# Routing products on whole 128x128 stationary tiles in a fused attention and two-stage expert kernel

## The chip, the cores and the metric

One core of one Trainium2 chip runs the whole kernel in one launch. The metric is device time in microseconds; the kernel before took 1211.03 us, the median of three runs.

## What is computed

The reference is an attention with two kinds of masks, then a layer of eight experts that each take exactly their share of tokens, then a layer of four experts that every token passes, mixed by given weights. The change touches the routing of the first expert layer alone:

```python
    logits = x @ w_gate                      # 2304 tokens, 8 experts
    order = np.argsort(-flat)
    ...
        if assigned[tok] >= 0 or counts[e] >= cap:      # cap = 2304 // 8 = 288
            continue
        assigned[tok] = e
    ...
    for e in range(E):
        mask = assigned == e
        h = np.maximum(x[mask] @ w1[e], 0.0)
        out[mask] = h @ w2[e]
```

## The kernel before, in words

Tokens lie as 128 partitions times 18 columns (NC). Routing goes in eight turns, g = 0 to 7. In each, `search` (line 552) finds the logit threshold at which the next expert fills up: every token's best remaining logit m and its one-hot expert oh (`best`, line 516), then rounds of a search over the bits of the threshold. A round compares m with up to 128 candidate thresholds (G, `reach`, line 529), counts per expert on TensorE how many tokens reach each candidate (line 595 in turn 0, 18 products; line 601 in turns 1 to 6, 9 products of two token columns each), lets VectorE count the candidates at which an expert is full (sat), spreads that to all partitions by a product with sat as stationary operand (line 608, in the last round followed by line 610), and sets the next bits. Turn 0 takes its first counts in the front already (`first_count`, line 543, product in line 545). Turns 0 to 6 have six rounds each; in turns 1 to 6 rounds one and two have 64 candidates of which 63 are counted (126 columns for two token columns), three more 31 (62 columns), the last 32 (64 columns). Turn 7 takes what is left without a search. Each turn ends with a prefix count (lines 655 and 656, both with a full 128x128 stationary tile), which gives each token its place.

`place` (line 677) turns places into a list of token indices: a one-hot W of 18 columns per token column, multiplied on TensorE with the one-hot O (line 696, 18 products), a copy to tk, and three fp32 products with K["rad"] (line 703, each issued as two), cast to idx. Then GpSimd gathers the tokens' rows (line 891), TensorE transposes them (line 908; line 915 in turn 0), and ScalarE and VectorE split them in a high and a low part (xh, xl) for the expert's products.

Stationary operands of the routing are narrow: 8 columns in line 545 and 595, 40 in line 601, 18 in line 696; in line 608 they stand on 8 partitions, in line 610 on 1, in line 703 on 18 partitions with 32 columns.

`experts` (line 750) issues the products of both expert layers (lines 971 and, later, 1201; all 128x128 stationary, moving 256, 288 or 512 columns in fp32r). The order on every engine is written out when the program is built. After each expert product `tick` (line 955) advances a planned TensorE time and lets the two chains, `chain_a` (searches) and `chain_b` (placements and gathers), emit their next piece when it is due. Routing products don't count in that planned time; VectorE operations count by their shapes. So the pieces of turns 1 to 7 stand between the expert products in one queue of TensorE, from about 160 to 610 us. Turn 0 runs before the first expert's products, between transposes of attention rows (lines 276 and 287) that are stored for the gather.

Of the kernel before, what the change touches and what calls it, by code (L numbers as in the profile page):

```python
# [18 lines left out]
FT = mybir.dt.float32  # L19
# [436 lines left out]
def route_consts(nc, cst):  # L456
    K = {}
    tok = cst.tile([128, NC], I32, name="tok")
    nc.gpsimd.iota(tok[:, :16], pattern=[[576, 4], [256, 2], [1, 2]], base=0, channel_multiplier=2)
    for b in range(4):  # L460
        nc.gpsimd.iota(tok[32 * b:32 * b + 32, 16:], pattern=[[1, 2]], base=576 * b + 512, channel_multiplier=2)
    vi = cst.tile([128, NC, 2], I32, name="vi")
    nc.vector.tensor_scalar(vi[:, :, 0], tok, 8, None, op0=OP.arith_shift_right)
    nc.vector.tensor_scalar(vi[:, :, 1], tok, 255, None, op0=OP.bitwise_and)
    K["vals"] = cst.tile([128, NC, 2], BF, name="vals")
    nc.vector.tensor_copy(K["vals"], vi)
    K["w8"] = cst.tile([128, 8], FT, name="w8")
    nc.gpsimd.iota(K["w8"], pattern=[[-1, 8]], base=8, channel_multiplier=0, allow_small_or_imprecise_dtypes=True)
    K["w8b"] = cst.tile([1, 8], BF, name="w8b")
    nc.gpsimd.iota(K["w8b"], pattern=[[-1, 8]], base=-8, channel_multiplier=0, allow_small_or_imprecise_dtypes=True)  # L470
    jj = cst.tile([128, 128], I32, name="jj")
    nc.gpsimd.iota(jj, pattern=[[1, 128]], base=0, channel_multiplier=0)
    K["jsh"], K["id8"] = {}, {}
    one_f = cst.tile([8, 8], FT, name="one_f")
    nc.gpsimd.memset(one_f, 1.0)
    i8 = cst.tile([8, 8], FT, name="i8")
    nc.gpsimd.affine_select(i8, one_f, pattern=[[-1, 8]], base=0, channel_multiplier=1, compare_op=OP.is_equal, fill=0.0)
    for nb, sh, first in ((7, 25, True), (6, 26, True), (6, 20, False), (5, 15, False), (5, 10, False), (5, 5, False), (5, 0, False)):
        n = 1 << nb
        t = cst.tile([128, n], I32, name=f"jsh{sh}")  # L480
        nc.vector.tensor_scalar(t, jj[:, :n], sh, None, op0=OP.logical_shift_left)
        if first:
            a = cst.tile([128, n], I32, name=f"ja{sh}")
            nc.vector.tensor_scalar(t, t, INT_MIN, None, op0=OP.bitwise_xor)
            nc.vector.tensor_scalar(a, t, 31, 0x7FFFFFFF, op0=OP.arith_shift_right, op1=OP.bitwise_and)
            nc.vector.tensor_tensor(t, t, a, OP.bitwise_xor)
            nc.vector.memset(t.bitcast(FT)[:, 0:1], -3.0e38)
        K["jsh"][sh] = t
        s = cst.tile([8, 8], BF, name=f"id8_{sh}")
        nc.vector.tensor_scalar(s, i8, 1.0 if first else float(1 << sh) if sh else 16.0, None, op0=OP.mult)  # L490
        K["id8"][sh] = s
    K["ones"] = cst.tile([128, 128], BF, name="ones")
    nc.gpsimd.memset(K["ones"], 1.0)
    K["ntri"] = cst.tile([128, 128], BF, name="ntri")
    nc.gpsimd.memset(K["ntri"], -1.0)
    nc.gpsimd.affine_select(K["ntri"], K["ntri"], pattern=[[-1, 128]], base=0, channel_multiplier=1, compare_op=OP.is_ge, fill=0.0)
    K["j32"] = cst.tile([128, 32], I32, name="j32")
    nc.gpsimd.iota(K["j32"], pattern=[[1, 32]], base=0, channel_multiplier=0)
    K["k9"] = cst.tile([128, 9], I32, name="k9")
    nc.gpsimd.iota(K["k9"], pattern=[[1, 9]], base=-32, channel_multiplier=0)  # L500
    K["zeros"] = cst.tile([128, 2 * NC], FT, name="zeros")
    nc.gpsimd.memset(K["zeros"], 0.0)
    radix = cst.tile([18, 3, 3, 2], FT, name="radix")
    nc.gpsimd.iota(radix, pattern=[[0, 9], [-255, 2]], base=256, channel_multiplier=0, allow_small_or_imprecise_dtypes=True)
    rsel = cst.tile([18, 3, 3, 2], FT, name="rsel")
    nc.gpsimd.affine_select(rsel, radix, pattern=[[-2, 3], [-6, 3], [-1, 2]], base=0, channel_multiplier=1, compare_op=OP.is_equal, fill=0.0)
    K["rad"] = cst.tile([18, 3, 3], FT, name="rad")
    nc.vector.tensor_reduce(K["rad"], rsel, AX.X, OP.add)
    K["first"] = [cst.tile([128, NC], FT, name="m0"), cst.tile([128, NC], FT, name="mw0"), cst.tile([128, NC, 32], BF, name="oh0"),
                  cst.tile([128, NC, 8], FT, name="eq0")]  # L510
    nc.vector.memset(K["first"][2], 0.0)
    K["cnt"] = cst.tile([8, 128], FT, name="cnt0")
    return K


# [24 lines left out]
    reach(nc, K["first"][0], K["jsh"][25].bitcast(FT), G, c0, c1, 128)  # L540


def first_count(nc, K, G, p, c0, c1):
    for c in range(c0, c1):
        nc.tensor.matmul(p[:8, :127], K["first"][2][:, c, :8], G[:, c - c0, 1:128], start=c == c0, stop=c == c1 - 1)
    if c0 == 0:
        nc.vector.tensor_copy(K["cnt"][:, :127], p[:8, :127])
    elif c0 < 14:
        nc.vector.tensor_tensor(K["cnt"][:, :127], p[:8, :127], K["cnt"][:, :127], OP.add)


def search(nc, K, wk, ps, L, g, S, out):
# [5 lines left out]
    if g < 7:  # L558
# [5 lines left out]
        for r, (nb, sh) in enumerate(rounds):  # L564
# [1 line left out]
            lo = 0 if sh == 0 else 1  # L566
            nxt = rounds[r + 1] if sh else None
            p = ps.tile([128, 128], FT, name="pa")
            sat = wk.tile([8, 1], BF, name="sat")
            junk = wk.tile([8, 128], FT, name="junk")  # L570
            if g == 0 and r == 0:
                G = wk.tile([128, 4, 128], BF, name="G")
# [7 lines left out]
            else:  # L580
# [11 lines left out]
                yield "d"  # L592
                if g == 0:
                    for c in range(NC):
                        nc.tensor.matmul(p[:8, lo:n], oh[:, c, :8], G[:, c, lo:n], start=c == 0, stop=c == NC - 1)
                    yield "p"
                    nc.vector.tensor_scalar(junk[:, lo:n], p[:8, lo:n], float(CAP), 0.0, op0=OP.is_ge, op1=OP.add, accum_out=sat)
                else:
                    pp = p[:, :2 * n].rearrange("p (a n) -> p a n", a=2)[:, :, lo:]
                    for c in range(0, NC, 2):  # L600
                        nc.tensor.matmul(pp[:40], oh[:, c:c + 2, :].rearrange("p a e -> p (a e)")[:, :40], G[:, c:c + 2, lo:n], start=c == 0, stop=c == NC - 2)  # L601
                    yield "p"
                    need = wk.tile([8, 64], FT, name="need")
                    nc.vector.tensor_scalar(need[:, lo:n], pp[32:40, 1], -1.0, float(CAP), op0=OP.mult, op1=OP.add)
                    nc.vector.scalar_tensor_tensor(junk[:, lo:n], pp[:8, 0], 0.0, need[:, lo:n], op0=OP.add, op1=OP.is_ge, accum_out=sat)
            yield "d"
            p = ps.tile([128, 8], FT, name="pa")
            nc.tensor.matmul(p, sat.to_broadcast([8, 128]), K["id8"][sh], start=True, stop=sh > 0)
            if sh == 0:
                nc.tensor.matmul(p, K["ones"][:1], K["w8b"], start=False, stop=True)  # L610
            yield "P"
            d = wk.tile([128, 1], I32, name="d", bufs=2)
            nc.vector.tensor_reduce(d, p, AX.X, OP.max)
# [63 lines left out]
def place(nc, K, wk, ps, out):  # L677

    pm = out["pm"]
    kj = wk.tile([128, 2, NC], I32, name="kj")  # L680
    nc.vector.tensor_scalar(kj[:, 0], pm, 5, None, op0=OP.arith_shift_right)
    nc.vector.tensor_scalar(kj[:, 1], pm, 31, None, op0=OP.bitwise_and)
    yield "q"
    O = wk.tile([128, NC, 32], BF, name="O")
    W9 = wk.tile([128, NC, 9], BF, name="W9")
    W = wk.tile([128, NC, 9, 2], BF, name="W")
    nc.vector.tensor_tensor(W9, K["k9"][:, None, :].to_broadcast([128, NC, 9]), kj[:, 0, :, None].to_broadcast([128, NC, 9]), OP.is_equal)
    pi = ps.tile([128, 32], FT, name="pb")
    for c0 in (0, 9):
        s = slice(c0, c0 + 9)  # L690
        yield "q"
        nc.vector.tensor_tensor(O[:, s], K["j32"][:, None, :].to_broadcast([128, 9, 32]), kj[:, 1, s, None].to_broadcast([128, 9, 32]), OP.is_equal)
        nc.vector.tensor_tensor(W[:, s], W9[:, s, :, None].to_broadcast([128, 9, 9, 2]), K["vals"][:, s, None, :].to_broadcast([128, 9, 9, 2]), OP.mult)
    yield "d"
    for c in range(NC):
        nc.tensor.matmul(pi[:18], W[:, c].rearrange("p k v -> p (k v)"), O[:, c], start=c == 0, stop=c == NC - 1)
    yield "p"
    tk = wk.tile([18, 32], FT, name="tk")
    nc.vector.tensor_copy(tk, pi[:18])
    yield "d"  # L700
    pi = ps.tile([128, 3], FT, name="pb")
    for b in range(3):
        nc.tensor.matmul(pi[32 * b:32 * b + 32], tk, K["rad"][:, b], start=True, stop=True)
    yield "p"
    idx = wk.tile([96, 3], I32, name="idx", bufs=2)
    nc.vector.tensor_copy(idx, pi[:96])
    out["idx"] = idx
# [673 lines left out]
```

## Time and profile before

| | us |
|---|---|
| median of 3 runs | 1211.03 |
| lowest and highest | 1208.41, 1212.58 |
| profiled execution, its time | 1208.96 |
| its span, first to last instruction | 1207.2 |
| TensorE busy in it (share of the span) | 1177.4 (98%) |
| VectorE | 853.9 (71%) |
| ScalarE | 621.8 (52%) |
| GpSimd | 422.9 (35%) |

PE is TensorE's products, PEld its weight loads, DVE VectorE, ACT ScalarE, POOL GpSimd, SP the engine that issues most DMAs. Records of products overlap and their ends are modelled, so the distance between starts tells more than their lengths. The span is what the trace shows; the median is over other executions of the same program.

### The profile page before, as it was taken

The page shows a single profiled execution, that of the slowest core. Times are in us where ns is not written, and L with a number is a line of the kernel's source. Part 1 is how long each engine was busy: PE and PEld are TensorE (multiplying, and loading weights), DVE is VectorE, ACT ScalarE, POOL GpSimd, SP SyncE. Part 2 cuts the span into 40 slices and gives each one's busy share as a digit, 9 for nine tenths or more (in the row PEclk, how much of TensorE's full clock was granted, in tenths as well). Part 3 has the DMA queues.
Part 4 walks back from the last instruction along what each step waited for, and adds up shares of the span by engine and source line. Part 5 has one row for each costly group of instructions (what it writes and reads, how often), then busy time and mean ns, then how long its engine had stood idle before and what let it go on. Part 6 is the DMA issues. An engine that isn't in the chain of part 4 may idle for free.

```text
span 1207.2 us, 24909 instructions
## 1 busy us (share of the span) xinstructions
PE 1177.4 (98%) x9088; PEld 1038.6 (86%) x9095; DVE 853.9 (71%) x2248; ACT 621.8 (52%) x1602; POOL 422.9 (35%) x453
## 2 busy tenths in 40 slices
PE   9999799999999999999999999999999999999997
PEld 6777588898888888899999988999888999899996
DVE  5777677777785877778765588767877766766673
ACT  5898455542441442455545455555555555555552
POOL 4343030100000101001012565565755556756553
PEclk9999899999999999999999999999999999999999
DMA  8761564553252452475665433333433333333320
GB/s 187 181 151 39 172 203 147 163 166 99 88 160 81 136 156 56 141 226 170 191 204 156 127 90 102 98 100 102 125 103 89 105 105 105 123 106 102 98 81 36
DMA packets 191955, 152.98 MB, mean 127 GB/s; under 512 B 27640, under 2 KB 158776, under 8 KB 191400
## 3 DMA queue, kind: packets, MB, share of 16 engines
q1 hardware_dynamic: 188664, 141.74, 40.2%
q0 software_dynamic: 3168, 9.65, 2.5%
q8 instruction: 71, 1.16, 0.4%
q14 instruction: 52, 0.43, 0.1%
HBM read 141.77 MB, written 9.58 MB: 125 GB/s over the span
## 4 chain that ended last, share of the span: by engine, by line
PE 82%; DVE 7%; issue 3%; ACT 3%; DMA 2%; POOL 2%; SPq 0%; POOLq 0%; DVEq 0%; ACTq 0%
PE o L971 35%; PE h L971 18%; PE h L1201 16%; DVE wl L746 3%; DMA raw<-in_moe_w_dram 2%; PE tr L164 2%; PE pt L222 1%; PE pa L601 1%; PE tr L153 1%; PE av L242 1%; PE s L186 1%; PE av L235 1%; ACT hh L864 1%; POOL wl L1190 1%; DVE u L746 1%
## 5 line engine op out<-in xcount | busy, mean ns | idle before, releaser
L746 DVE TENSOR_TENSOR wl<-raw,wh 128x512 fp32r<-128x512 f32 x352 | 272.0, 804 | 4.6 <-ACT wh L844 3.8
L971 PE MATMUL o<-wl,hh 128*128 128x512 f32 x576 | 227.8, 395 | 0.0
L971 PE MATMUL o<-wh,hh 128*128 128x512 f32 x576 | 227.7, 395 | 0.0
L971 PE MATMUL o<-wh,hl 128*128 128x512 f32 x576 | 226.5, 393 | 0.0
L864 ACT ACTIVATE hh<-h 128x256 fp32r<-128x256 f32 (+1 forms) x208 | 81.7, 393 | 241.2 <-PE h L971 221.4
L844 ACT CAST wh<-raw 128x512 fp32r<-128x512 f32 x272 | 160.0, 619 | 59.8 <-DMA raw<-in_moe_w_dram 57.7
L1190 POOL TENSOR_TENSOR wl<-raw,wh 128x512 fp32r<-128x512 f32 x96 | 122.5, 1298 | 194.8 <-ACT wh L1189 194.7
L746 DVE SCALAR_TENSOR_TENSOR hl<-h,hh 128x256 fp32r<-128x256 f32 (+1 forms) x208 | 89.8, 432 | 103.6 <-ACT hh L864 102.4
L891 POOL DMA_INDIRECT xg<-xd,idx x24 | 26.3, 1095 | 367.0 <-DVE idx L746 285.0
L971 PEld LDWEIGHTS o<-wh,hl 128*128 128x128 f32 x576 | 108.6, 188 | 23.3
L1201 PE MATMUL h<-hold,wh 128*128 128x256 f32 x640 | 120.9, 282 | 1.4 <-DVE u L746 1.1
L1201 PEld LDWEIGHTS h<-hold,wh 128*128 128x128 f32 x640 | 107.9, 188 | 15.8 <-DVE u L746 2.8
L746 DVE SCALAR_TENSOR_TENSOR hl<-u,hh 128x256 fp32r<-128x256 f32 x144 | 83.0, 576 | 46.5 <-ACT hh L864 46.5
L1176 ACT CAST wh<-sums 128x512 fp32r<-128x512 f32 x96 | 59.8, 622 | 106.9 <-POOL sums L1164 70.6
L971 PEld LDWEIGHTS o<-wl,hh 128*128 128x128 f32 x576 | 108.6, 189 | 6.0
L971 PEld LDWEIGHTS o<-wh,hh 128*128 128x128 f32 x576 | 108.5, 188 | 6.1
L864 ACT ACTIVATE hh<-u 128x256 fp32r<-128x256 f32 x144 | 59.9, 416 | 103.3 <-DVE u L746 103.2
L746 DVE TENSOR_TENSOR u<-h,u 128x256 f32<-128x256 f32 x144 | 60.2, 418 | 62.9 <-PE h L1201 55.5
L746 DVE TENSOR_TENSOR wl<-sums,wh 128x512 fp32r<-128x512 f32 x96 | 74.7, 779 | 36.7 <-ACT wh L1176 36.7
L1201 PE MATMUL h<-hold,wl 128*128 128x256 f32 x320 | 89.8, 281 | 0.0
L971 PE MATMUL h<-xh,wh 128*128 128x288 f32 x256 | 76.1, 297 | 0.0
L971 PE MATMUL o<-hh,wl 128*128 128x288 f32 x256 | 76.0, 297 | 0.0
(271 smaller groups left out, 2927.2 us busy)
## 6 DMA issues: line engine op xcount, KB each, us to landing
raw<-in_moe_w_dram SPq DMA_DIRECT2D x464, 256.0 KB
vl<-in_v_dram SPq DMA_DIRECT2D x16, 192.0 KB
ql<-in_q_dram SPq DMA_DIRECT2D x4, 576.0 KB
kl<-in_k_dram SPq DMA_DIRECT2D x4, 576.0 KB
qs<-in_q_dram SPq DMA_DIRECT2D x3, 576.0 KB
ks<-in_k_dram SPq DMA_DIRECT2D x3, 576.0 KB
xd<-y SPq DMA_DIRECT2D x2, 576.0 KB
xd<-hl SPq DMA_DIRECT2D x5, 192.0 KB
```

Source lines behind the costliest of these rows:

```text
L153: nc.tensor.transpose(p[:, 72 * a:72 * a + 72], src[:, r:r + 2, :].rearrange("p r d -> p (r d)"), ident[:72, :72])
L164: nc.tensor.matmul(p[64 * x:64 * x + 64, 96 * t:96 * t + 96], src[:, 2 * hp + x, 3 * a + t, :], ident[:96, :96], start=True, stop=True)
L186: nc.tensor.matmul(out[:rows], lt, rt, start=True, stop=True)
L222: nc.tensor.transpose(p[:keys, rows * j:rows * j + rows], T["p"][:rows, j, :keys], ident[:rows, :rows])
L746: return f(*args, **kw)
L844: nc.scalar.copy(c["h"][:, sl], c["raw"][a])
L864: nc.scalar.activation(hi, src, AF.Relu)
L891: nc.gpsimd.indirect_dma_start(out=xg[:, k, :], out_offset=None, in_=xd, in_offset=bass.IndirectOffsetOnAxis(ap=idx[:, k:k + 1], axis=0))
L971: nc.tensor.matmul(out, a, b, start=start, stop=stop)
L1176: nc.scalar.copy(S["W"][nm][0], src[nm]())
L1190: nc.gpsimd.tensor_tensor(l, r, h.bitcast(FT), OP.subtract)
L1201: mmx = lambda o, a, b, first, lastm, n: (nc.tensor.matmul(o, a, b, start=first, stop=lastm, skip_group_check=True), tick(n / 2315 + 0.009))
```

## The change

Every narrow stationary operand becomes 128 partitions by 128 columns. In `search` the columns of oh are taken four token columns at a time (32 each), of which the results read only the first; oh gets three more token columns. sat becomes a constant tile of 128 partitions that is zero but for the first 8; the small constants are made on 128 partitions (zero outside their old part; a fill is added for w8b). In `place` W and tk become constant tiles with zeros behind (and before) their old part, filled once by GpSimd in the first placement; line 703's three products become three accumulating ones over a shifting window of tk. Moving columns, VectorE's operations and the order of the pieces stay.

```diff
-    K["w8b"] = cst.tile([1, 8], BF, name="w8b")
-    nc.gpsimd.iota(K["w8b"], pattern=[[-1, 8]], base=-8, channel_multiplier=0, allow_small_or_imprecise_dtypes=True)
+    K["w8b"] = cst.tile([128, 8], BF, name="w8b")
+    nc.gpsimd.memset(K["w8b"], 0.0)
+    nc.gpsimd.iota(K["w8b"][:1], pattern=[[-1, 8]], base=-8, channel_multiplier=0, allow_small_or_imprecise_dtypes=True)
...
-    K["first"] = [cst.tile([128, NC], FT, name="m0"), cst.tile([128, NC], FT, name="mw0"), cst.tile([128, NC, 32], BF, name="oh0"),
+    K["first"] = [cst.tile([128, NC], FT, name="m0"), cst.tile([128, NC], FT, name="mw0"), cst.tile([128, NC + 3, 32], BF, name="oh0"),
...
+    K["sat"] = cst.tile([128, 1], BF, name="sat")
+    nc.vector.memset(K["sat"], 0.0)
...
+def whole(oh, c):
+    return oh[:, c:c + 4, :].rearrange("p a e -> p (a e)")
...
-        nc.tensor.matmul(p[:8, :127], K["first"][2][:, c, :8], G[:, c - c0, 1:128], start=c == c0, stop=c == c1 - 1)
+        nc.tensor.matmul(p[:, :127], whole(K["first"][2], c), G[:, c - c0, 1:128], start=c == c0, stop=c == c1 - 1)
...
-            sat = wk.tile([8, 1], BF, name="sat")
+            sat = K["sat"][:8]
...
-                        nc.tensor.matmul(p[:8, lo:n], oh[:, c, :8], G[:, c, lo:n], start=c == 0, stop=c == NC - 1)
+                        nc.tensor.matmul(p[:, lo:n], whole(oh, c), G[:, c, lo:n], start=c == 0, stop=c == NC - 1)
...
-                        nc.tensor.matmul(pp[:40], oh[:, c:c + 2, :].rearrange("p a e -> p (a e)")[:, :40], G[:, c:c + 2, lo:n], start=c == 0, stop=c == NC - 2)
+                        nc.tensor.matmul(pp, whole(oh, c), G[:, c:c + 2, lo:n], start=c == 0, stop=c == NC - 2)
...
-            nc.tensor.matmul(p, sat.to_broadcast([8, 128]), K["id8"][sh], start=True, stop=sh > 0)
+            nc.tensor.matmul(p, K["sat"].to_broadcast([128, 128]), K["id8"][sh], start=True, stop=sh > 0)
             if sh == 0:
-                nc.tensor.matmul(p, K["ones"][:1], K["w8b"], start=False, stop=True)
+                nc.tensor.matmul(p, K["ones"], K["w8b"], start=False, stop=True)
...
-    W = wk.tile([128, NC, 9, 2], BF, name="W")
+    if "W" not in K:
+        K["W"] = wk.tile([128, NC * 18 + 110], BF, name="W")
+        nc.gpsimd.memset(K["W"][:, NC * 18:], 0.0)
+        K["tk"] = wk.tile([128, 224], FT, name="tk")
+        nc.gpsimd.memset(K["tk"], 0.0)
+    W = K["W"][:, :NC * 18].rearrange("p (c k v) -> p c k v", c=NC, v=2)
...
-        nc.tensor.matmul(pi[:18], W[:, c].rearrange("p k v -> p (k v)"), O[:, c], start=c == 0, stop=c == NC - 1)
+        nc.tensor.matmul(pi, K["W"][:, 18 * c:18 * c + 128], O[:, c], start=c == 0, stop=c == NC - 1)
     yield "p"
-    tk = wk.tile([18, 32], FT, name="tk")
-    nc.vector.tensor_copy(tk, pi[:18])
+    nc.vector.tensor_copy(K["tk"][:18, 96:128], pi[:18])
...
-        nc.tensor.matmul(pi[32 * b:32 * b + 32], tk, K["rad"][:, b], start=True, stop=True)
+        nc.tensor.matmul(pi, K["tk"][:, 96 - 32 * b:224 - 32 * b], K["rad"][:, b], start=b == 0, stop=b == 2)
```

## Rows read from the trace of the kernel before

**Rows 1.** Stage table: length, then busy PE, PEld, DVE, ACT, POOL; clock; DMA

```profile
160.00:610.00 450.00, 444.74 (x3321) 400.14 (x3321) 336.07 (x944) 197.69 (x425) 31.80 (x32) 1.00 0.48 145
```

**Rows 2.** Chain of waits in 160 to 610 us, shares of the stage by line

```profile
by line: PE h L971 41.5%; PE o L971 40.7%; PE pa L601 3.3%; DMA raw<-in_moe_w_dram 3.2%; DVE wl L746 1.9%; ACT wh L844 1.6%; PE pb L908 1.1%; DVE G L746 0.9%; PE pb L696 0.8%; PE pa L608 0.8%; issue 0.8%; DVE xl L746 0.6%; DVE hl L746 0.6%; 
```

**Rows 3.** Timeline of PE, one line 608 product: start, length, instruction (us)

```profile
167.44 0.29 PE L971 MATMUL h<-xl,wh 128*128 128x288 f32 x1
167.67 0.17 PE L608 MATMUL pa<-id,sat 8*128 8x8 bf16 x1
167.78 0.40 PE L971 MATMUL h<-xh,wl 128*128 128x288 f32 x1
168.01 0.29 PE L971 MATMUL h<-xh,wh 128*128 128x288 f32 x1
168.14 0.29 PE L971 MATMUL h<-xl,wh 128*128 128x288 f32 x1
```

**Rows 4.** Timeline of PE, the full-tile pair of lines 655 and 656

```profile
515.01 0.29 PE L971 MATMUL h<-xh,wh 128*128 128x288 f32 x1
515.14 0.19 PE L655 MATMUL pa<-st,ntri 128*128 128x36 bf16 x1
515.18 0.18 PE L656 MATMUL pa<-cum,ones 128*128 128x36 bf16 x1
515.21 0.38 PE L971 MATMUL h<-xl,wh 128*128 128x288 f32 x1
515.43 0.29 PE L971 MATMUL h<-xh,wl 128*128 128x288 f32 x1
```

**Rows 5.** Timeline of PE, a group of line 601 with 126 columns

```profile
171.58 0.29 PE L971 MATMUL h<-xh,wh 128*128 128x288 f32 x1
171.81 0.68 PE L601 MATMUL pa<-G,oh 128*40 128x126 bf16 x9
...
172.65 0.29 PE L971 MATMUL h<-xh,wl 128*128 128x288 f32 x1
```

**Rows 6.** Timeline of PE, a group of line 601 with 62 columns

```profile
176.51 0.30 PE L971 MATMUL o<-hh,wl 128*128 128x288 f32 x1
176.74 0.44 PE L601 MATMUL pa<-G,oh 128*40 128x62 bf16 x9
...
177.34 0.29 PE L971 MATMUL o<-hl,wh 128*128 128x288 f32 x1
```

**Rows 7.** Timeline of PE, a group of line 696

```profile
338.31 0.29 PE L971 MATMUL o<-hh,wl 128*128 128x288 f32 x1
338.52 0.61 PE L696 MATMUL pb<-O,W 128*18 128x32 bf16 x18
...
339.30 0.29 PE L971 MATMUL h<-xl,wh 128*128 128x288 f32 x1
```

**Rows 8.** Timeline of PE, a group of line 703

```profile
341.02 0.30 PE L971 MATMUL o<-hh,wl 128*128 128x288 f32 x1
341.24 0.23 PE L703 MATMUL pb<-rad,tk 18*32 18x3 f32 x6
...
341.64 0.29 PE L971 MATMUL o<-hl,wh 128*128 128x288 f32 x1
```

**Rows 9.** Timeline of PE in the front, line 340

```profile
59.07 0.31 PE L340 MATMUL xr<-four,lg 128*128 128x16 f32 x2
```

**Rows 10.** Groups of instructions, 160 to 610 us, line 908: busy us, mean ns | idle before it, releaser

```profile
L908 PE MATMUL pb<-ident,xg 96*128 96x96 f32 x72 | 10.2, 250 | 4.3 <-DVE xl L746 4.3
```

**Rows 11.** Timeline of all engines, end of the first placement; brackets: idle before, releaser

```profile
145.02 0.41 PE L696 MATMUL pb<-O,W 128*18 128x32 bf16 x9 [0.20 <-DVE W L746]
...
146.04 0.16 DVE L746 CAST idx<-pb 96x3 int32<-96x3 f32 x1 [0.39 <-PE pb L703]
...
147.16 1.03 POOL L891 DMA_INDIRECT xg<-xd,idx  x1 [30.17 <-DMA raw<-in_moe_w_dram]
```

**Rows 12.** Timeline of POOL at the start, a small fill

```profile
3.81 0.13 POOL L502 MEMSET zeros<- 128x36 f32 x1
```

More of the change, by code (lines that the diff above doesn't have):

```diff
@@ L473, in route_consts @@
     K["jsh"], K["id8"] = {}, {}
-    one_f = cst.tile([8, 8], FT, name="one_f")
+    one_f = cst.tile([128, 8], FT, name="one_f")
     nc.gpsimd.memset(one_f, 1.0)
-    i8 = cst.tile([8, 8], FT, name="i8")
+    i8 = cst.tile([128, 8], FT, name="i8")
     nc.gpsimd.affine_select(i8, one_f, pattern=[[-1, 8]], base=0, channel_multiplier=1, compare_op=OP.is_equal, fill=0.0)
@@ L488, in route_consts @@
         K["jsh"][sh] = t
-        s = cst.tile([8, 8], BF, name=f"id8_{sh}")
+        s = cst.tile([128, 8], BF, name=f"id8_{sh}")
         nc.vector.tensor_scalar(s, i8, 1.0 if first else float(1 << sh) if sh else 16.0, None, op0=OP.mult)
@@ L502, in route_consts @@
     nc.gpsimd.memset(K["zeros"], 0.0)
-    radix = cst.tile([18, 3, 3, 2], FT, name="radix")
+    radix = cst.tile([128, 3, 3, 2], FT, name="radix")
     nc.gpsimd.iota(radix, pattern=[[0, 9], [-255, 2]], base=256, channel_multiplier=0, allow_small_or_imprecise_dtypes=True)
-    rsel = cst.tile([18, 3, 3, 2], FT, name="rsel")
+    rsel = cst.tile([128, 3, 3, 2], FT, name="rsel")
     nc.gpsimd.affine_select(rsel, radix, pattern=[[-2, 3], [-6, 3], [-1, 2]], base=0, channel_multiplier=1, compare_op=OP.is_equal, fill=0.0)
-    K["rad"] = cst.tile([18, 3, 3], FT, name="rad")
+    K["rad"] = cst.tile([128, 3, 3], FT, name="rad")
     nc.vector.tensor_reduce(K["rad"], rsel, AX.X, OP.add)
-    K["first"] = [cst.tile([128, NC], FT, name="m0"), cst.tile([128, NC], FT, name="mw0"), cst.tile([128, NC, 32], BF, name="oh0"),
+    K["first"] = [cst.tile([128, NC], FT, name="m0"), cst.tile([128, NC], FT, name="mw0"), cst.tile([128, NC + 3, 32], BF, name="oh0"),
                   cst.tile([128, NC, 8], FT, name="eq0")]
```

## The prediction, made before the changed kernel was run

> **What bounds the kernel now.** I read the stage table first. Between 160 and 610 us, where seven of the eight searches and placements run among the products of the experts, TensorE is busy 444.74 of 450 us at full granted clock, VectorE 336.07 [rows 1]. Then the chain of waits of that stage: 41.5% and 40.7% of it are the experts' products, and the routing's own products stand in it too, line 601 with 3.3% (14.9 us), lines 696 and 608 with 0.8% each [rows 2]. Line 608's 0.8% is 3.6 us, 36 rounds at 0.10 us, which is the 0.11 us from its start to the next product's [rows 3]: nearly all of its rounds lie on the chain. So TensorE's time in the routing counts here. The rest of the chain is mostly weight loads from memory (3.2%), VectorE and ScalarE.
>
> What a routing product costs is read from starts in the timeline, since records overlap. Products of 288 columns start 0.13 us apart. With one line 608 product among them (8 rows x 128 columns stationary) the last product before starts at 167.44 and the second after at 168.01: 0.57 us where two steps are 0.26, so it adds 0.31 us [rows 3]. It starts 0.10 us later than its turn, and the second product after is late by another 0.10. Now the kernel's own full-tile pair, lines 655 and 656, same types, 128x128 stationary, 36 columns: from 515.01 to 515.43 is 0.42 us, so **two** of them add 0.16 us. The first comes on its turn (0.13), the second 0.04 later, the next product 0.03 after that [rows 4]. The partial tile costs a wait on both sides that the full one doesn't.
>
> **The change part by part.** A full-tile product alone is taken at 0.16 - 0.04 = 0.12 us, each further one in a group at the larger of 0.04 us (the pair's step) and its own streaming. Line 601's groups of nine last 0.68 us with 126 columns [rows 5] and 0.44 with 62 [rows 6]; with the last record near 0.19, as 36 columns have [rows 4], the short ones step by (0.44 - 0.19) / 8 = 0.03 us, the long ones by 0.03 more, 0.06. Counts are from the loops: six searches of six rounds after 160 us, two rounds of 126 columns and four of 62 or 64 in each; seven placements.
>
> Saturation product (608), 36 rounds: 0.31 becomes 0.12, saves 0.19 each, 6.8 us. Line 610, in one round of six, keeps its step and is counted at nothing: it stands behind 608 in the same group.
>
> Line 601, 126 columns, 12 groups: 171.58 to 172.65 is 1.07, less 0.26, adds 0.81 [rows 5]. After: 0.12 + 8 x 0.06 + 0.03 for the longer last one = 0.63. Saves 0.18 each, 2.2 us.
>
> Line 601, 62 or 64 columns, 24 groups: 176.51 to 177.34 is 0.83, adds 0.57 [rows 6]. After: 0.12 + 8 x 0.04 = 0.44. Saves 0.13 each, 3.1 us. Here the wider load takes part back (0.04 for 0.03).
>
> Line 696, 18 products, 7 placements: 338.31 to 339.30 is 0.99, adds 0.73 [rows 7]. After: 0.12 + 17 x 0.04 = 0.80. **Costs** 0.07 each, 0.5 us.
>
> Line 703, six issues of three fp32 products: 341.02 to 341.64 is 0.62, adds 0.36 [rows 8]. No row shows a stream of full fp32 tiles with 3 columns. Two of line 340 (full fp32, 16 columns) take 0.31 us together [rows 9], one full fp32 product lasts 0.25 [rows 10], so their step is 0.06. After: 0.12 + 5 x 0.06 = 0.42, costs 0.06 each, 0.4 us. Bounds are 0.04 (the bf16 pair, rows 4) and 0.11 (a load after a drain, rows 3): from a gain of 0.3 to a loss of 2.2 us. I take the value next to line 340, which has the same type and tile.
>
> Sum: 6.8 + 2.2 + 3.1 - 0.5 - 0.4 = **11.2 us** of TensorE's time after 160 us. Not all of it reaches the end: where the chain runs through loads, ScalarE and VectorE, TensorE waits anyway, as at the transposes of gathered tokens (4.3 us idle behind VectorE's xl [rows 10]). TensorE's lines make 41.5 + 40.7 + 3.3 + 1.1 + 0.8 + 0.8 = 88% of that chain [rows 2], so I take 0.88 x 11.2 = 9.9 us. Bounds are 11.2 (all of it) and some 3.5 (rival two).
>
> The first search and placement, before 155 us, I cost at nothing, between a loss and a gain of 0.8 us. Five saturation products save up to 5 x 0.19 and the groups of line 595 give some back by their loads, as line 696 does. In the placement a stationary tile now reaches into later columns of W, so 16 products instead of 9 wait for the second half of W (the record of those nine is 0.41 us [rows 11]): 7 more at 0.04 to 0.11 us and wider ones, and the three fp32 products, make the indices 0.5 to 1.6 us later. Hidden behind: the index cast ends at 146.20 and the first gather starts at 147.16, released by a DMA that landed [rows 11], so 0.96 us of delay costs nothing; without that cover it goes straight into the gather, on which the first expert waits. The line 545 counts save at most a wait or two in the front. The two fills of the placement's pads come on GpSimd, which is idle for 30.17 us before that gather [rows 11]; the added fill at the start is one like line 502's, 0.13 us [rows 12], ahead of masks that nobody needs in the first microseconds. Were these covers gone, each costs its 0.13. No wait on VectorE's queue is added: it reads the same corners of the results, and the order written by the pacing doesn't count routing products.
>
> The profiled execution took 1208.96 us, span 1207.2; the median is 1211.03, 2.1 above it. 1208.96 - 9.9 = 1199.1, on the median **1201.1 us**.
>
> **The rivals.** One: the load of 128 columns isn't wholly covered. The pair's 0.04 is one step, not a stream of nine. With a load covered only in part, a step of 126 columns lies between 0.06 (covered) and 0.10 (0.06 + 0.04). The page TensorE: Matmul & The Clock Gate of the Trainium skill, section Back-to-back issue gap, gives some 81 ns for a sustained load and product of 128 columns; no row here shows such a stream. At 0.08, and 0.055 and 0.05 for the shorter ones, line 601 saves 12 x 0.02 + 24 x 0.01 = 0.5, line 696 loses 7 x 0.24 = 1.7, line 703 0.4, 608 keeps its 6.8: 5.2 x 0.88 = 4.6 us, 1206.5. For it: nine different loads in a row. Against: the expert products load 128 fp32 columns for each 0.13 us step without a trace of it [rows 3].
>
> Two: VectorE and the weight loads take over. They have 0.75 of the stage busy and own stretches of the chain. If two thirds of the gain is waited away again at xl and at the loads, 3.7 us is left, 1207.3. Against: those stretches begin with a product that itself comes earlier.
>
> Three, the other side: a wide load costs what it costs after a drain, 0.11 us each [rows 3], in every group of the search and the placement. Then a long group is 0.12 + 8 x 0.11 + 0.03 = 1.03, loses 0.22 x 12 = 2.6; a short one 1.00, loses 0.43 x 24 = 10.3; line 696 1.99, loses 1.26 x 7 = 8.8; line 703 0.31 x 7 = 2.2; with 6.8 gained that is 17.1 lost, 15 on the chain, 1226. It decides from a step of 0.071 us, where the sum is zero. The rule that speaks for it is in the Trainium skill, TensorE: Matmul & The Clock Gate, section LDWEIGHTS (loading the stationary operand): a load's time goes by its columns, 1.2 in a nanosecond, by which 128 would take an estimated 107 ns and 40 take 33. The pair's step of 0.04 [rows 4] speaks against it, so I hold to the sum of 11.2.
>
> Four: the change doesn't do what it says, because the wait belongs to the change of type (bf16 among fp32) and not to the tile. Then wider loads cost 2 to 3 us and nothing is saved, 1213.5. Rows 4 have the same change of type and no wait on entry.
>
> **How the numbers follow.** Forecast 0.73, rival one 0.10, two 0.08, three 0.05, four 0.04. About 0.3%, 3.6 us, is what a measurement can tell from no change. Faster: 0.73 + 0.10 + half of two = 0.87; same: the other half and rival four, 0.08; slower: rival three, 0.05. Range: low 1196.5, with the whole 11.2 us, the upper bounds of line 703 and of the first placement and an execution as far under the median as the profiled one; high 1207.5, which takes in rivals one and two.
>
> **What would show it.** Right: line 608 starting 0.12 to 0.13 us after the product before it, the next product 0.03 behind; groups of line 601 near 0.51 us with 62 columns; line 696's group longer than 0.61 us; TensorE's idle time at xl a little larger than 4.3. Wrong: line 601's steps over 0.07 us, a start still 0.10 late, or the same stage length with longer waits for raw and xl.

## The result and the profile after

The changed kernel takes 1197.42 us (median of 4 runs, 1195.12 to 1198.43), the kernel before, run beside it, 1211.2. The ratio is 0.9894, 95% interval 0.9877 to 0.991: faster by 1.1%, where 0.8% was forecast. The profiled execution took 1198.43 us, the longest of the four.

The page of the changed kernel, span and busy time:

```profile
span 1196.7 us, 24923 instructions
...
PE 1167.4 (98%) x9095; PEld 1040.1 (87%) x9095; DVE 852.7 (71%) x2249; ACT 622.0 (52%) x1602; POOL 424.1 (35%) x456
```

The stage table of 160 to 610 us, columns as in [rows 1]:

```profile
160.00:610.00 450.00, 444.07 (x3402) 410.94 (x3402) 343.57 (x959) 203.57 (x438) 35.07 (x34) 1.00 0.50 152
```

TensorE is as full as before and still at full granted clock, but 3402 of its products now lie in the same 450 us, against 3321 [rows 1]. It does the same work with less waiting between its products.

The timeline of PE in the changed kernel (start, length, instruction, us): a saturation product (now line 615), a count of 126 columns and one of 62 (line 608), a placement (708) and its index products (714), each with its neighbours among the experts' products:

```profile
168.56 0.29 PE L982 MATMUL h<-xl,wh 128*128 128x288 f32 x1
168.69 0.18 PE L615 MATMUL pa<-id,sat 128*128 128x8 bf16 x1
168.73 0.38 PE L982 MATMUL h<-xh,wl 128*128 128x288 f32 x1
168.95 0.29 PE L982 MATMUL h<-xh,wh 128*128 128x288 f32 x1
...
177.27 0.29 PE L982 MATMUL o<-hh,wl 128*128 128x288 f32 x1
177.41 0.44 PE L608 MATMUL pa<-G,oh 128*128 128x62 bf16 x9
177.68 0.38 PE L982 MATMUL o<-hh,wh 128*128 128x288 f32 x1
177.90 0.29 PE L982 MATMUL o<-hl,wh 128*128 128x288 f32 x1
...
247.23 0.29 PE L982 MATMUL o<-hh,wh 128*128 128x288 f32 x1
247.37 0.68 PE L608 MATMUL pa<-G,oh 128*128 128x126 bf16 x9
247.85 0.38 PE L982 MATMUL o<-hl,wh 128*128 128x288 f32 x1
248.07 0.29 PE L982 MATMUL o<-hh,wl 128*128 128x288 f32 x1
...
334.18 0.29 PE L982 MATMUL o<-hh,wl 128*128 128x288 f32 x1
334.32 0.61 PE L708 MATMUL pb<-O,W 128*128 128x32 bf16 x18
334.78 0.38 PE L982 MATMUL h<-xh,wh 128*128 128x288 f32 x1
335.00 0.29 PE L982 MATMUL h<-xl,wh 128*128 128x288 f32 x1
...
336.71 0.30 PE L982 MATMUL o<-hh,wl 128*128 128x288 f32 x1
336.85 0.73 PE L714 MATMUL pb<-rad,tk 128*128 128x3 f32 x6
337.43 0.38 PE L982 MATMUL o<-hh,wh 128*128 128x288 f32 x1
337.65 0.30 PE L982 MATMUL o<-hl,wh 128*128 128x288 f32 x1
```

Read by starts, as before. The saturation product starts on its turn, 0.13 us behind 168.56, and the next product 0.04 later; from 168.56 to 168.95 is 0.39, so it adds 0.13 where it added 0.31 [rows 3]. The two counts, read the same way, add 0.63 less 0.26, 0.37, where it was 0.57, and 0.84 less 0.26, 0.58, where it was 0.81 [rows 5, 6]. The records' lengths tell nothing of this: the 62-column group lasts 0.44 in both kernels, and so does the 126-column one with 0.68 [rows 5, 6]. What went are the waits before and behind them. The placement, which I thought would grow, adds 334.18 to 335.00 less 0.26, 0.56, against 0.73 [rows 7]. The index products alone grew: 336.71 to 337.65 is 0.94, adds 0.68, against 0.36 [rows 8].

Done for all groups between 160 us and the last placement, medians of the added time in us (for the last column, times the count). A group's added time runs from the start of the product before it to the start of the second product behind it, less the steps that these two neighbours have without it (0.13 us with 288 columns, 0.12 with 256, 0.23 with 512):

| group | count | before | predicted | changed | saved, us |
|---|---|---|---|---|---|
| saturation | 36 | 0.305 | 0.12 | 0.126 | 6.4 |
| counts, 126 columns | 12 | 0.81 | 0.63 | 0.57 | 2.9 |
| counts, 62 or 64 | 24 | 0.57 | 0.44 | 0.367 | 4.9 |
| placement | 7 | 0.74 | 0.80 | 0.555 | 1.3 |
| index products | 7 | 0.38 | 0.42 | 0.687 | -2.1 |

Together 13.4 us of TensorE's time, for the 11.2 of the prediction. To see what of it reaches the end I take the stretch from the first count after the front to the last index product, by the first and last starts of their lines. Those of the kernel before, then of the changed one:

```profile
L601 PE MATMUL pa<-G,oh x324: 193/193/233, 164.3 to 504.4; 128*40 128x62 bf16 x84, 128*40 128x126 bf16 x54, 128*40 128x64 bf16 x24
...
L703 PE MATMUL pb<-rad,tk x48: 167/187/209, 145.7 to 607.7; 18*32 18x3 f32 x48
```

```profile
L608 PE MATMUL pa<-G,oh x324: 189/193/230, 165.5 to 494.0; 128*128 128x62 bf16 x84, 128*128 128x126 bf16 x54, 128*128 128x64 bf16 x24
...
L714 PE MATMUL pb<-rad,tk x48: 166/252/373, 147.2 to 597.1; 128*128 128x3 f32 x48
```

443.4 us (164.3 to 607.7) became 431.6 (165.5 to 597.1): 11.8 of the 13.4 us arrive. Behind the stage the two traces stay a constant distance apart: 10.6 us at the last index product, 10.5 at the end of the span. What the stage's chain of waits and TensorE's waits show of the rest, first the chain's shares by line, then who TensorE waited for (us in total, times, longest):

```profile
by line: PE h L982 39.3%; PE o L982 38.4%; DMA raw<-in_moe_w_dram 6.9%; PE pa L608 2.4%; DVE wl L757 1.8%; ACT wh L855 1.6%; PE pb L919 1.1%; issue 0.9%; DVE G L757 0.9%; PE pb L714 0.8%; PE pb L708 0.7%; DVE xl L757 0.7%; DVE hl L757 0.6%; 
```

```profile
PE pb L919 <- DVE xl L757: 3.7, 6, 1.2
PE pa L615 <- DVE junk L757: 0.8, 1, 0.8
...
PE o L982 <- DVE hold L757: 0.5, 1, 0.5
```

Saturation no longer stands in the chain's list and the counts fell from 3.3% to 2.4% [rows 2]; weight loads rose from 3.2% to 6.9%, so the chain now passes through them more often, yet TensorE hardly idles more: its waits over 50 ns in the stretch sum to 5.9 us against 5.3. The wait at xl was 4.3 [rows 10] and is 3.7 here; new are one for the search's own VectorE result ahead of a saturation product (0.8) and one at the combination of the experts' outputs (hold, 0.5).

### The profile page after: what moved, and what is told of

Its sections match the earlier page's. It is cut to its first block, busy times and chain, and to the rows that moved or that the text cites. A ratio compares the mean times of both kernels' runs of the same rounds, so it can differ in the third digit from the quotient of the medians.

```text
span 1196.7 us, 24923 instructions
## 1 busy us (share of the span) xinstructions
PE 1167.4 (98%) x9095; PEld 1040.1 (87%) x9095; DVE 852.7 (71%) x2249; ACT 622.0 (52%) x1602; POOL 424.1 (35%) x456
## 4 chain that ended last, share of the span: by engine, by line
PE 79%; DVE 6%; DMA 6%; issue 3%; ACT 3%; POOL 2%; SPq 1%; POOLq 0%; DVEq 0%; ACTq 0%
PE o L982 34%; PE h L982 17%; PE h L1212 17%; DMA raw<-in_moe_w_dram 3%; DVE wl L757 2%; PE tr L164 1%; PE pt L222 1%; PE av L242 1%; PE pa L608 1%; DMA kl<-in_k_dram 1%; DMA ks<-in_k_dram 1%; DMA vl<-in_v_dram 1%; POOL wl L1201 1%; PE s L186 1%; ACT hh L875 1%
## 5 line engine op out<-in xcount | busy, mean ns | idle before, releaser
L982 PE MATMUL h<-xl,wh 128*128 128x288 f32 x256 | 76.0, 297 | 0.0
```

The source lines that it names most:

```text
L982: nc.tensor.matmul(out, a, b, start=start, stop=stop)
```

## The experiments

The ratio of every run is to the kernel before, timed beside it. Of each edit the lines that matter are shown; `...` stands for the rest. "Stage" is the stretch just defined, 443.4 us before.

**The changed kernel again, twice,** with no edit, to see how far stage and time scatter.

> The changed kernel once more, unedited. If the landing of early loads varies from execution to execution, its front (start of the first expert product, 155.5 us before, 1.3 later in the changed kernel's first trace) comes out somewhere between -1 and +3 us of the first trace's, and the stage from 160 to 507 us again 12 us shorter. If the change itself delays the front (one more fill at the start, other addresses), the same 2.3 us stand at 42 us again. Time 1195 to 1199.

> The changed kernel, beside the two versions of its index products on the same chip. 1196 to 1199; stage from 165.5 to 610 us (places of before) 11 to 12 us shorter.

Measured: 1198.39 us, ratio 0.9908 (0.9889 to 0.9928), and 1196.51, 0.9896 (0.9868 to 0.9924). Stages 432.1 and 431.8: shorter by 11.3 and 11.6. The stage repeats to 0.5 us, while the front before it moves by nearly 3 us between executions of one kernel: the stage begins at 165.5, 162.8 and 162.9 us. In the first of these TensorE's granted clock fell to 0.50 (1.2 GHz) in the front, behind a wait for a load of vl that is shown further down. The stretch of 36.7 to 40.1 us in it, columns as in [rows 1]; in both repeats it has 1.00:

```profile
36.70:40.10 3.40, 3.40 (x26) 2.43 (x24) 1.36 (x2) 1.15 (x6) 0.65 (x1) 0.50 0.84 196
```

So the stage is the better ruler for the parts.

**Only the saturation products padded** (lines 608 and 610 of the kernel before, with their constant tile). Counts and placement as before; against the kernel before:

```diff
-            nc.tensor.matmul(p, sat.to_broadcast([8, 128]), K["id8"][sh], start=True, stop=sh > 0)
+            nc.tensor.matmul(p, K["sat"].to_broadcast([128, 128]), K["id8"][sh], start=True, stop=sh > 0)
...
```

> Only lines 608 and 610 padded, counts and placement as before. By starts in the changed kernel's trace a saturation product adds 0.13 us and not 0.31: 36 x 0.18 = 6.4 us of TensorE's time. If it reaches the end as in the whole change (11.5 to 12.0 us of 13.3 there), 5.6 us faster than before. If one of two neighbours in a round hides behind the other, less than 4.

Measured: 1203.71 us, ratio 0.995 (0.9932 to 0.9969); stage 437.5, shorter by 5.9 for 6.4 saved on TensorE. The largest term of the prediction (6.8) stands alone, near its size.

**Only the counts padded** (lines 545, 595 and 601). Saturation and placement as before; against the kernel before:

```diff
-                        nc.tensor.matmul(pp[:40], oh[:, c:c + 2, :].rearrange("p a e -> p (a e)")[:, :40], G[:, c:c + 2, lo:n], start=c == 0, stop=c == NC - 2)
+                        nc.tensor.matmul(pp, whole(oh, c), G[:, c:c + 2, lo:n], start=c == 0, stop=c == NC - 2)
...
```

> Only the counts padded (lines 545, 595, 601): long groups 0.57 for 0.81, short ones 0.37 for 0.57: 12 x 0.24 + 24 x 0.20 = 7.7 us of TensorE's time, 6.8 at the end. With the step of 0.04 that the prediction took it would be 5.3 and 4.7.

Measured: 1203.54 us, ratio 0.995 (0.9935 to 0.9965); stage also 437.5, shorter by 5.9 for 7.8 saved, and 6.8 expected. Half of the missing 1.9 us is waited away at the place that the prediction named. Of TensorE's waits:

```profile
PE pb L915 <- DVE xl L753: 5.2, 6, 1.8
```

That is 0.9 us over the 4.3 before, and not in every version: in the three traces of the changed kernel it is 3.7, 4.3 and 3.8.

**Saturation and counts padded, placement as before** (the two edits above together).

> Saturation and counts padded, placement as before. If the two add up: 14.1 us of TensorE's time, 12.4 at the end, so as fast as the whole change or 0.5 us faster (the placement's two edits are worth 1.3 and -2.1). If the waits share something, clearly less than the sum of the two runs before.

Measured: 1195.87 us, ratio 0.991 (0.9877 to 0.9942); stage 431.0, shorter by 12.4. The two parts alone make 5.9 + 5.9 = 11.8, so they add up. With the placement padded too the stage is 11.3 to 11.8 shorter, so the placement's edit as a whole loses 0.6 to 1.1 us: its 18 products gain 1.3, the index products lose 2.1.

**Index products narrow again** (18 x 32, fp32, from a tile tk of its own for each placement), all else as changed; against the changed kernel:

```diff
-        nc.tensor.matmul(pi, K["tk"][:, 96 - 32 * b:224 - 32 * b], K["rad"][:, b], start=b == 0, stop=b == 2)
+        nc.tensor.matmul(pi[32 * b:32 * b + 32], tk, K["rad"][:18, b], start=True, stop=True)
...
```

> Index products back on 18 partitions and 32 columns, all else as changed. In the changed kernel's trace a group of six adds 0.69 us, before it added 0.38. If TensorE's time in the stage reaches the end, 7 x 0.30 = 2.1 us faster than the changed kernel, 1195.3. If VectorE and the loads had taken over, no difference.

> Index products narrow in fp32 as before the change: 0.37 us a group, 2.2 us of TensorE's time, 1.9 us faster than the changed kernel, and 1.1 behind the bf16 version.

Measured: 1195.02 us, ratio 0.9873 (0.9853 to 0.9894), and again 1195.11, 0.9885 (0.9858 to 0.9912). Both stages 429.8, shorter by 13.6. Against the changed kernel that is 1.8 to 2.3 us, what the index products lost on TensorE (2.1). The profiled execution of the repeat (1209.95 us) began its stage only at 178.8 us: its granted clock was 0.50 from 38.6 to 65.9 us. The stage itself is not touched by that. The narrow products differ from the padded ones in more than their width: the three write to three different strips of 32 partitions of the result, and their issues start 0.007 us apart in two threes, while the padded ones all add up in one place. How narrow fp32 products would fare that follow each other in one strip no run shows.

**Index products padded, but in bf16**, against the changed kernel. They put an index together from digits and the factors 1 and 256, which bf16 holds:

```diff
-    K["rad"] = cst.tile([128, 3, 3], FT, name="rad")
+    K["rad"] = cst.tile([128, 3, 3], BF, name="rad")
...
-        K["tk"] = wk.tile([128, 224], FT, name="tk")
+        K["tk"] = wk.tile([128, 224], BF, name="tk")
```

> Index products full 128x128 but in bf16 (the numbers, at most 255 and 256, are exact in it): three issues and not six, and a load that steps at 0.03 to 0.04 us and not 0.11. A group adds 0.12 + 2 x 0.04 = 0.20 us and not 0.69: 7 x 0.49 = 3.4 us faster than the changed kernel, 1194. If the 0.11 belongs to the shifted window and not to fp32, the group stays over 0.4 and it is under 2 us.

> Index products full in bf16. Their groups add 0.18 us and not 0.69, 3.5 us of TensorE's time; at 0.87 of it 3.0 us faster than the changed kernel beside it. If VectorE and the loads close in, under 2.

Measured: 1195.59 us, ratio 0.9886 (0.9863 to 0.9909), and 1196.24, 0.9881 (0.9854 to 0.9907). The timeline of PE, the three index products:

```profile
336.06 0.30 PE L983 MATMUL o<-hh,wl 128*128 128x288 f32 x1
336.20 0.23 PE L715 MATMUL pb<-rad,tk 128*128 128x3 bf16 x3
336.29 0.38 PE L983 MATMUL o<-hh,wh 128*128 128x288 f32 x1
336.51 0.29 PE L983 MATMUL o<-hl,wh 128*128 128x288 f32 x1
```

336.06 to 336.51 is 0.45, less 0.26 adds 0.19, where the same tile in fp32 adds 0.69 and the narrow one 0.38. The stages are 14.9 and 12.4 us shorter. The second lost its 2.5 to the clock and to waits. TensorE waited 1.8 us for xl ahead of 231.57, and from 232.4 to 235.9 us the granted clock was half of full speed; products with 512 columns step by 0.43 us there, by 0.23 elsewhere. That stretch in the second trace, then in the first:

```profile
232.40:235.90 3.50, 3.50 (x18) 3.02 (x17) 1.99 (x4) 1.39 (x4) 0.00 (x0) 0.51 0.21 62
```

```profile
232.40:235.90 3.50, 3.50 (x29) 3.24 (x26) 2.70 (x9) 1.14 (x4) 0.00 (x0) 1.00 0.48 136
```

By starts this costs some 1.6 us, and the waits are 0.8 larger (7.2 us for 6.4). Against the changed kernel on the same chip the medians are 2.8 and 0.3 us better, where 3.4 and 3.0 were expected: the second fell short of it. The narrow index was expected 1.1 behind this version and came out 1.1 ahead. Over all runs the medians are 1197.2 us for the changed kernel (16 runs), 1196.0 for this one (12) and 1195.1 for the narrow index (13). Both look better than the change by one or two us, with intervals that overlap; which of the two is better the runs don't tell.

**All tiles 72 wide instead of 128, then 64, then 120.** These separate the wait from the load, and the tile from its type: the types are the same in all of them. Saturation takes that many rows, the others that many columns (the index products 96, 96 and 120). The edit of 72 against the changed kernel:

```diff
-                        nc.tensor.matmul(pp, whole(oh, c), G[:, c:c + 2, lo:n], start=c == 0, stop=c == NC - 2)
+                        nc.tensor.matmul(pp[:72], whole(oh, c)[:, :72], G[:, c:c + 2, lo:n], start=c == 0, stop=c == NC - 2)
...
-            nc.tensor.matmul(p, K["sat"].to_broadcast([128, 128]), K["id8"][sh], start=True, stop=sh > 0)
+            nc.tensor.matmul(p, K["sat"][:72].to_broadcast([72, 128]), K["id8"][sh][:72], start=True, stop=sh > 0)
...
```

> All padded operands cut: counts and placement on 72 columns, saturation on 72 partitions, indices on 96 columns. If what counts is that the products stay in one tile shape (over half of the array), no wait returns: sat still adds 0.13 us, groups of the counts 0.57 and 0.37, placement 0.56, index products 0.69 less 5 x 0.03 by fewer columns; time as changed, within 1 us, 1 faster at most. If a load of the full 128 columns is what is quick, steps grow to some 0.06 us: short groups 0.24 longer (24 of them), placement 0.6 longer (7), about 10 us slower than the changed kernel. If padding needs all 128 for the shape, the waits of before return, 1209 or more.

Measured: 1198.01 us, ratio 0.9899 (0.9876 to 0.9922); stage 433.1. That is the changed kernel's time within 1 us, as expected. The timeline of PE at a saturation product of 72 rows:

```profile
178.74 0.29 PE L982 MATMUL h<-xh,wl 128*128 128x288 f32 x1
178.87 0.18 PE L615 MATMUL pa<-id,sat 72*128 72x8 bf16 x1
178.91 0.38 PE L982 MATMUL h<-xh,wh 128*128 128x288 f32 x1
179.13 0.29 PE L982 MATMUL h<-xl,wh 128*128 128x288 f32 x1
```

> As the run with 72 columns and 72 partitions, with 64 in their place, indices on 96 columns. If a tile of at most half the array is another shape, the waits of before return: sat adds 0.30 us, groups of the counts 0.8 and 0.6, placement over 0.74; time that of before plus 1 us for the indices. If only small tiles (32) are, all as with 72, 1198.

Measured: 1212.34 us, ratio 1.0027 (1.0012 to 1.0041); stage 445.1, longer than before by 1.7, where 1 was expected for the index products; on TensorE these add 1.2, and the placement 1.0. A saturation product with 64 rows:

```profile
167.17 0.29 PE L982 MATMUL h<-xl,wh 128*128 128x288 f32 x1
167.46 0.18 PE L615 MATMUL pa<-id,sat 64*128 64x8 bf16 x1
167.56 0.40 PE L982 MATMUL h<-xh,wl 128*128 128x288 f32 x1
167.80 0.29 PE L982 MATMUL h<-xh,wh 128*128 128x288 f32 x1
```

This is the pair that decides. With 72 rows the product comes on its turn and adds 0.13; with 64 it comes late on entry (0.29) and on exit, and adds 0.37 here, 0.31 in the median. Eight more rows of zeros take the whole wait away, in the same types. Counts and placement behave alike by columns: at 64 a long count adds 0.82 and a placement 0.88, at 72 they add 0.56 and 0.71.

> As the run with 72, with 120 columns and 120 partitions everywhere, indices on 120 columns too. With 72 columns the placement's products stepped by 0.035 us, with the full 128 by 0.025. If a bf16 load goes by its columns and only the full width of 128 is loaded in a quicker way, 120 columns step by 0.035 x 120 / 72 = 0.058: short groups 8 x 0.029 longer than in the changed kernel (24), placement 17 x 0.033 (7), 9.5 us of TensorE's time, some 8 us slower than the changed kernel, 1205. If what is over half the array is quick as such and 72 was slow for another reason, steps of 0.025 to 0.035 and the changed kernel's time. No wait at the change of tile in either case.

Measured: 1207.63 us, ratio 0.9982 (0.9973 to 0.9991); stage 438.8. Some 1205 was expected. A 120-wide tile has no wait either, and yet 7.0 us of the stage come back against 128; the rest of the distance to the changed kernel lies in the front, the stage begins at 166.3 us here. The timeline of PE at a placement:

```profile
337.50 0.29 PE L982 MATMUL o<-hh,wl 128*128 128x288 f32 x1
337.63 1.11 PE L708 MATMUL pb<-O,W 128*120 128x32 bf16 x18
338.60 0.38 PE L982 MATMUL h<-xh,wh 128*128 128x288 f32 x1
```

18 products last 1.11 us with 120 columns, 0.61 with 128. By starts (from the group's to the next product's, divided by 18) a step is 0.97 / 18 = 0.054 against 0.46 / 18 = 0.026; by the single instructions' starts 0.055 and 0.025. The records of the loads point the same way. Loads of the counts by line, count and duration (ns, min/median/max), of this kernel and then of the changed one, there with the index products' too:

```profile
L608 PEld LDWEIGHTS <-oh x324: 130/135/136, 166.1 to 500.9; 128*120 128x120 bf16 x162
```

```profile
L608 PEld LDWEIGHTS <-oh x324: 95/98/103, 165.5 to 493.9; 128*128 128x128 bf16 x162
...
L714 PEld LDWEIGHTS pb<-rad,tk x48: 187/192/333, 147.2 to 597.1; 128*128 128x128 f32 x48
```

The record of a full bf16 tile's load lasts 98 ns, of the one eight columns narrower 135, of the full fp32 one 192.

The saved TensorE time of each version (its groups' medians times their counts, as in the table above) beside the shortening of its stage, in us:

| version | TensorE | stage |
|---|---|---|
| saturation only | 6.4 | 5.9 |
| counts only | 7.8 | 5.9 |
| both | 14.2 | 12.4 |
| changed (three traces) | 13.4 | 11.8, 11.3, 11.6 |
| index narrow (two) | 15.5 | 13.6, 13.6 |
| index in bf16 (two) | 16.9 | 14.9, 12.4 |
| 72 wide | 12.7 | 10.3 |
| 120 wide | 5.8 | 4.6 |
| 64 wide | -3.1 | -1.7 |

In every version that gains, 73 to 92% of TensorE's saving shortens the stage; the 73% is the trace whose clock fell.

## Why the prediction was right, and which terms were off

**The mechanism was right.** A narrow tile among full ones costs a wait before it and one behind, and padding takes both away: seen in the timeline and cut free by the pair of 64 and 72 rows. The wait is some 0.18 us for the two sides together (0.305 less 0.126). The page TensorEngine Tiling (Array Packing) of the Trainium skill, section Key Properties, says that a change of the array's tiling mode (not of the tile) drains TensorE. The trace agrees as far as it goes: it shows the wait and its edge between 64 and 72, not the mode.

**Rival four** (it is the type) fell with that pair. **Rival three** (each wide load 0.11) fell for bf16: the full tile steps by 0.025 to 0.03 under 32 and 62 columns, far under the point of 0.071 from which it would have decided. Its price is real elsewhere: at full fp32 tiles, where the index products pay it. **Rival one** (0.08 at 126 columns) fell: the step there is 0.056, as with the narrow tile before. **Rival two** took what the table shows, 12 to 16% in the changed kernel, not two thirds. (It spoke of VectorE and the loads with 0.75 of the stage busy; that is VectorE's share, the DMA's is 0.48 [rows 1]. And what it leaves is 3.7 us, where the bounds of the sum say some 3.5.)

**The share that reaches the end**, taken as 0.88 from TensorE's lines in the chain, was 11.3 to 11.8 of 13.4, 0.84 to 0.88. That it would be lost at xl was not borne out in the changed kernel (3.7 for 4.3), only with the counts alone (5.2). Summed over all groups, and not by medians, TensorE saves 12.9 us. Its larger waits (5.9, 6.4 and 6.2 us in the three traces, against 5.3) take 0.7 to 1.2 of them, and the experts' own products away from the groups, 2486 steps, take 0.4 more than before; with that the sum closes. Why these steps grew is open. That 0.88 came so near is in part luck: the listed lines of TensorE make 83, 82 and 77% of the chain in the three traces of the changed kernel, whose stages differ by 0.5 us, so such a share doesn't measure what arrives.

**Mis-sized: "the larger of 0.04 us (the pair's step) and its own streaming".** The pair [rows 4] shows the first step of a group, and that one is 0.039 in the changed kernel too; the later ones are 0.029 at 62 columns and 0.025 at 32. So the short counts saved 4.9 us, not 3.1, and the placement, booked as a loss of 0.5, gained 1.3.

**Mis-sized: line 703's step, "the value next to line 340".** Taken as 0.06, it measured 0.112, the upper of the two bounds (0.11). The index products cost 2.1 us instead of 0.4. The 0.06 was the length of a pair's records in rows 9 less a single one in rows 10, and that one was no full tile with 16 columns: it stands on 96 rows and moves 96 columns. A pair's length also doesn't show the step of a longer stream: in the changed kernel the first step of an index group is 0.027 us and the later ones 0.112. And the narrow fp32 products before hid the price, since they start 0.007 us apart in their three strips. The two errors have opposite signs, 3.6 us and 1.7, and with 0.3 of the rest more they make the 2.2 us by which the sum was short; that they partly cancel is luck. Of the 3.7 us by which 1201.1 lay over the measured time, 1.9 are the stage (9.9 for 11.8). The other 1.8 are less than the scatter of the front (2.8 us between traces of the changed kernel), and no run tells more of them.

**The signs.** Of those named for being right, the first came: the saturation product starts 0.13 us behind the one before it, and the next 0.04 later. The other three didn't: the short counts' records stayed at 0.44 us, not 0.51, the placement's at 0.61, and the idle time at xl did not grow. The first two hung on the step of 0.04, the third on the share that is lost. No sign of being wrong came.

**The front, costed at nothing:** the end of the first placement, on the timeline of all engines of the changed kernel:

```profile
146.27 0.61 PE L708 MATMUL pb<-O,W 128*128 128x32 bf16 x16 [0.39 <-DVE W L757]
...
148.70 0.16 DVE L757 CAST idx<-pb 96x3 int32<-96x3 f32 x1 [1.53 <-PE pb L714]
...
149.15 1.04 POOL L902 DMA_INDIRECT xg<-xd,idx  x1 [21.85 <-DMA raw<-in_moe_w_dram]
```

The products that wait for the second half of W are 16 instead of 9, and the index cast starts 2.43 us behind the first of them, for 1.02 before [rows 11]: 1.4 later, inside the 0.5 to 1.6 predicted. Both stretches ran at a granted clock of 0.50, which the terms of the prediction, read at full clock, didn't reckon with. The gather starts 0.29 us after the cast ends, for 0.96 before, and the same 0.29 in both repeats, so the cover is used up, and some 0.7 us of the delay go on to the gather. Whether the front as a whole lost or gained can't be told from traces that scatter by 2.8 us. That W itself comes 1.25 us later here is not the change: in this execution the front waited for a load. The chain of waits in the front, of this execution and then of the changed kernel's first repeat:

```profile
27.48 9.02 DMA vl<-in_v_dram
36.54 0.56 PE av L242 x6
```

```profile
35.38 0.61 PE av L242 x16
```

The repeat, with the same instructions, passes there 1.2 us earlier and does not wait for that load; behind the wait comes the stretch at half clock shown with the repeats.

## What to carry to other kernels

Where TensorE is what the kernel waits for, a small stationary tile in a stream of full ones costs some 0.2 us in waits around its group: pad it beyond half of the array, and a bf16 one all the way to 128 columns, with zeros or with whatever lies next in memory if nobody reads those results. Leave narrow fp32 tiles that write to strips of their own as they are, or make them bf16 where the values allow, since the step of full fp32 tiles grows with their columns. And take a step from the starts in a stream like the one to come: a pair shows the first step only, which was too dear for bf16 and too cheap for fp32.

## What the runs showed of the hardware that was not expected

The wait has an edge between 64 and 72 rows or columns: the saturation product adds 0.31 us with 8 rows as with 64, and 0.13 with 72 as with 120 and 128. Between the two nothing was tried.

The load of a bf16 tile does not grow evenly with its columns. Steps of the placement's stream are 0.035 us at 72 columns, 0.055 at 120 and 0.025 at 128: the full tile is the cheapest of the three, and as cheap as the 18 columns before. In fp32 the steps of the index products do grow, 0.085 at 96, 0.105 at 120 and 0.112 at 128. The page TensorE: Matmul & The Clock Gate of the Trainium skill has both halves. Its section Weight-path perf modes — Fast Weight Load (FWL) and DoubleRow gives the fast load to 128 weights of a type other than fp32, with which the drop from 120 to 128 agrees. Its section LDWEIGHTS (loading the stationary operand) has the columns divided by 1.2 in ns, an estimated 107 for 128, near the 112 of fp32; for bf16 at 120 columns it would be an estimated 100, and the 55 measured decides.
